# Attention and mixing kernel: a tile's keys in one stretch of 160 columns, its values in two transfers, and a new written order

## The chip, the cores and the metric

The kernel runs on one core of one Trainium2 chip. The metric is the device time of one execution in microseconds (us), as a median over runs; one execution was also taken with the hardware profiler. TensorE is called PE here, its weight loads PEld, VectorE DVE, ScalarE ACT, GpSimd POOL and SyncE SP.

## What is computed

Sparse attention over batch 4, heads 8, sequence 768, head size 64, then a mixing block on the result:

```python
k_sum = k.reshape(B, H, nb, block, D).max(axis=3)        # block 32, nb 24
v_sum = v.reshape(B, H, nb, block, D).mean(axis=3)
mask_l = np.abs(pos[:, None] - pos[None, :]) < window    # window 16
scores_s = scale * np.einsum('bhsd,bhnd->bhsn', q, k_sum) + np.log(block)
scores_all = np.concatenate([scores_l_m, scores_s], axis=-1)
...
x = attention output, (B, S, H * D)
theta = x @ w_theta
yr = np.einsum('ts,bsd->btd', w_tok_r, x * np.cos(theta))
yi = np.einsum('ts,bsd->btd', w_tok_i, x * np.sin(theta))
u = x + yr + yi
out = u + np.maximum(u @ w_ch, 0.0)
```

A query sees its 15 neighbours on each side and the 24 block summaries; all else is masked away.

## The kernel before

The work is laid down as a list of operations, one after the other with what each reads and writes: the attention prepass of a batch (`prepass`: maxima of the keys on DVE, sums of the values by matmuls or by DVE), 24 attention tiles of 128 queries (`att_tile`), the theta product and the sines of each tile (`theta_tile`), the mix over tokens (`mix_step` for batches 0 and 1, `mix_fast` with seven products for batches 2 and 3) and the channel product (`out_batch`). PE runs these in turn; attention and theta of later tiles lie between mix products of earlier ones. Before any of it PE multiplies zeros for some 7.6 us (L381).

The order is not found at run time: `ORDER` (L54 to L143) names every operation by its number, in the order of issue, with a letter where another engine than the cheapest takes it (d DVE, g POOL). Each engine takes its instructions in the order of that list, and SP issues all transfers in it, one after the other, waiting for each one's buffer.

One attention tile takes two halves (g) of 64 queries. A half sees 24 block summaries and NL local keys, its 64 queries with HALO 15 on each side, 94 in all, so NK is 118. In `att_tile` (L481) the tile `k` holds for each of 4 head pairs and both halves these 118 columns, and behind them the queries. For batch 0 the local keys are copied from the whole keys in on-chip memory (`zu`, L506), one copy for each half and each two pairs; for batches 1 to 3 one transfer from `qg` brings local keys and queries (L529). The summaries are copied in at L515 and L519. The values `v` come in one transfer (L498) with both halves side by side; their 24 summaries stand above them, copied at L501. Then come the scores on PE (L538, two PSUM tiles `s`), the masked minimum on DVE (L574), the exponential on ACT (L578), a transpose on PE of each half's rows (L587), a copy of the turned weights `e` by ACT or DVE (L593), the product with `v` on PE (L561), and the division (L602 to L611). The PSUM tiles `pa` are shared by value sums, transposes and block products, so these wait for each other's copies.

The value sums of batch 0 are twelve matmul records at L452, from three transfers `x<-vn`; ACT copies the result at L475 (`vs`). The theta weights (`wth`) arrive as 64 bit floats and are turned to 32 bit ones in five steps (L403 to L414) on ACT, POOL and DVE, into tiles `xl` and `xh`; then they are scaled (L1031, L1032). Lines L763 are sums of quarters, on `f` for weights and on `zu` for the mix of batches 2 and 3.

Of the kernel before, what the change touches and what calls it, by code (L numbers as in the profile page):

```python
# [23 lines left out]
HALO = WIN - 1  # L24
# [6 lines left out]
VL = 96  # L31
# [23 lines left out]
27 23 25 15 31 39 17 24 29 99 44 28 33 0g 1g 2 35 78 3 45 4 186 40 85 26 193 43 8g 5 6g 9 30 10 11g 18 19 7g 194 20 21 22 32  # L55
12 48g 47 14 46 49 50 13 190g 237g 100 101g 34 239 59 63 235 51 60 52 64 61 65 238g 192 36 92 54 58 56 53 79 55 102 62 187 57
103 37 38g 104 105d 66 691d 67 80 81 82 42g 188g 83 191 68 195 41 291g 69d 70 196 189g 240g 84 71 86 87g 293 199 106 107 198
197 204 206 294g 207 200 203 205 685g 241 72 75d 289 73 210 76 208 74d 202 77d 88 93 223 236 201 211 209 347g 242 245 249 94
224 243 244 345g 247 89 212 213 215 214 246 225 248 216 117 95 220 90 96 91d 97 346g 250 397 348g 98 226 217d 251 252 108 253
218 221 254 227 256 219d 118g 292g 222d 122 119 228 123 255 258 257 124 229 230 689g 120 259 260 295 261 296 269 121 262 419g  # L60
125 231 109 298 270 263d 232 302 126 233 398 266 343 264 271 304 405 272 687g 273 274 290 399 128 692g 307 267 281 265d 311
268d 275 297 306 110 282 305 299 421g 301 309 276 349 285g 300 303 310 406 308 129g 350 352 234g 353 312 130 277 354 131 313
283 323 315 400 111 416 314 133 316 351 358 409 324 325 420 418 284 360 287g 278 317 362 134g 355 135 356 364 132 326 136 327
357 359 363 137 328 279g 344 401 288g 280 361 365 329 320d 403 422 318 321 319d 322d 410 431 366 367 138 686g 434 438 330 433
335 368d 337 331 417 377 688g 402 432 601g 369 332 404 378d 370 116 139g 338 476 690g 423 426 430 477 371d 374d 424 372 437
375 379 425 429 373d 376d 380 140 411 381 334 407 141 428 142 286g 113 16 427 439 436 435 527 440 441 442 478 602 382 172
333g 412 443 383 479 482 408 528 447d 444d 487 445 489 336 143 491 389 144g 448 112 384 173g 446 449d 488 524 486 490 153 413
494 493 145 414 174 146 492 114 391 450 473 483 480 484 481 485 415g 529 147 495 525 115 148 390 175 385 526 392 149g 386 154
475 127 451d 530 474 150 496 155 497 151 498 452 176 453 454 455 152 156 158 387 157 456 499 177 727 533 457 500 532 388g
503d 572 501 504 159g 178 538 458 459 502d 464 460g 506 466 540 505d 165 467 507 539 508 693 509 537 531 535 510 536 543 534  # L70
160 541 542 545 694 544 697 511 695 728 166g 167 179 462 512 161 546 547 168 573 162 169 696 463g 465 163 180 698 549 513 170
548d 164 514 515 699 181 171 550 182 516 518 608 522 554 183 523 700g 393 519 520 184 729 521 574 551 517g 575 561 341g 607
582 584 394g 576 461g 559 731 588 701 555 702 185 585 730 637 571 580 560 733 562 557 719 552 553 577 558g 732 579 581 703
1238 563 583 556 768 578 713g 734 569 565 771 589 586 342 609 339g 340g 769 590 587 720 567 591 592 704 564 638g 735 593 603
# [207 lines left out]
def attn_moe(tc, qg, vg, kT, vT, vn, wth, wtr, wti, wch, out, tune=TUNE):  # L282
# [69 lines left out]
    for g in range(2):  # L352
        local = lambda g=g: masks(slice(g * QT, (g + 1) * QT), slice(NB, NK))
        keep(local, [[0, 3], [1, NL]], 3 * NL, 0, -1, ALU.is_ge, far, (cs, "mask"))
        keep(local, [[0, 3], [-1, NL]], 3 * NL, 2 * HALO, 1, ALU.is_ge, far, (cs, "mask"))
# [798 lines left out]
```

## Time and profile before

| what | us |
|---|---|
| median of 3 runs | 426.37 |
| lowest, highest | 426.08, 429.6 |
| the profiled execution | 425.32 |
| its span, first to last instruction | 423.6 |
| PE, PEld, DVE, ACT, POOL busy | 413.3, 343.9, 356.3, 298.1, 207.4 |

The profiled execution's own time is the one to compare with sums made from its rows; its span is what the views cover. A matmul's end is modelled, so where PE counts as busy it may still not be at its pace; the start of the next run of matmuls says how long one took. An engine's idle time matters where PE waits behind it.

### The profile page before, as it was taken

The numbers are of one execution on the slowest core, as the hardware profiler recorded it, in microseconds if no ns is written. First come the engines' busy times: TensorE is split into PE (matmuls) and PEld (weight loads), VectorE is DVE, ScalarE is ACT, GpSimd is POOL, SyncE is SP. The second block draws the span as 40 slices with busy tenths as digits, with TensorE's granted clock in tenths as the row PEclk, the third lists the DMA queues.
The fourth block names the chain that finished last, engine by engine and source line by source line (L and its number), as shares of the span: only waits on it lengthen the run. The fifth ranks groups of instructions, "written<-read, shape, count | busy, mean of one in ns | idle before, by whom it ended". The sixth has DMA issues, their size and how long they took to land.

```text
span 423.6 us, 10058 instructions
## 1 busy us (share of the span) xinstructions
PE 413.3 (98%) x3626; PEld 343.9 (81%) x3626; DVE 356.3 (84%) x963; ACT 298.1 (70%) x609; POOL 207.4 (49%) x211
## 2 busy tenths in 40 slices
PE   8789999999999999999999999999999999999996
PEld 3356666578888888888888899898889999999996
DVE  3799999998797896787778787776887899999996
ACT  2899999997588886878779976685564547465230
POOL 3435562329833545875755876835515411133241
PEclk9999999999999999999999999999999999999999
DMA  8999799567869799777896998998788599111355
GB/s 294 351 351 319 256 384 285 157 212 193 273 181 245 177 261 277 223 241 230 227 271 166 310 248 244 303 267 249 182 242 336 192 349 305 50 39 45 124 209 183
DMA packets 95234, 100.07 MB, mean 236 GB/s; under 512 B 41936, under 2 KB 80848, under 8 KB 95184
## 3 DMA queue, kind: packets, MB, share of 16 engines
q1 hardware_dynamic: 95184, 99.43, 76.0%
q8 instruction: 28, 0.46, 0.4%
q14 instruction: 22, 0.18, 0.1%
HBM read 75.82 MB, written 23.59 MB: 235 GB/s over the span
## 4 chain that ended last, share of the span: by engine, by line
PE 88%; DVE 7%; ACT 2%; issue 1%; DMA 1%; DVEq 0%; SPq 0%; ACTq 0%
PE m L735 23%; PE m L851 20%; PE t L677 11%; PE c L956 6%; PE pa L561 6%; PE m L956 5%; PE s L538 5%; PE t L672 4%; PE pa L587 3%; PE t L381 2%; PE t L956 1%; DMA v<-vg 1%; DVE e L574 1%; DVE x L975 1%; DVE f L763 1%
## 5 line engine op out<-in xcount | busy, mean ns | idle before, releaser
L851 PE MATMUL m<-wt,hl 128*128 128x384 f32 x504 | 93.0, 339 | 0.3
L851 PEld LDWEIGHTS m<-wt,hl 128*128 128x128 f32 x504 | 87.2, 188 | 3.5 <-issue 0.5
L735 PE MATMUL m<-wt,hl 128*128 128x512 f32 x480 | 89.4, 340 | 0.0
L735 PEld LDWEIGHTS m<-wt,hl 128*128 128x128 f32 x480 | 74.2, 188 | 11.6 <-issue 0.3
L578 ACT ACTIVATE e<-e,st 128x118 f32<-128x118 f32 x192 | 64.4, 389 | 10.6 <-DVE st L574 7.3
L574 DVE CUSTOM_DVE_ANT_0 e<-s,cs 128x118 f32<-128x118 f32 x192 | 45.6, 271 | 7.1 <-PE pa L561 4.5
L320 POOL TENSOR_TENSOR hl<-zu,hl 128x512 fp32r<-128x512 f32 x24 | 33.1, 1386 | 27.8 <-ACT hl L311 8.5
L677 PE MATMUL t<-wth,xh 128*128 128x512 f32 x144 | 45.8, 399 | 0.0
L707 POOL TENSOR_TENSOR zu<-xn,zu 128x512 f32<-128x512 f32 x24 | 32.9, 1381 | 21.2 <-DVE wt L414 10.0
L311 ACT CAST hl<-zu 128x512 fp32r<-128x512 f32 x43 | 26.1, 619 | 16.4 <-PE m L851 9.9
L561 PEld LDWEIGHTS pa<-v,e 118*64 118x64 f32 x768 | 24.6, 137 | 9.7 <-issue 3.4
L320 DVE TENSOR_TENSOR hl<-zu,hl 128x512 fp32r<-128x512 f32 x38 | 28.3, 751 | 3.0 <-ACT hl L311 2.9
L561 PE MATMUL pa<-v,e 118*64 118x65 f32 x768 | 28.0, 224 | 2.7 <-ACT xh L1031 1.0
L677 PEld LDWEIGHTS t<-wth,xh 128*128 128x128 f32 x144 | 25.2, 188 | 4.5
L677 PE MATMUL t<-wth,xl 128*128 128x512 f32 x72 | 28.4, 394 | 0.0
L763 POOL TENSOR_TENSOR zu<-zu 128x512 f32<-128x512 f32 x14 | 18.8, 1357 | 16.2 <-DVE hl L320 10.9
L763 POOL TENSOR_TENSOR f<-f 128x192 f32<-128x192 f32 x26 | 17.4, 670 | 18.2 <-DVE f L763 11.2
L538 PE MATMUL s<-k 64*64 64x118 f32 x768 | 25.7, 266 | 0.6 <-PE pa L561 0.6
L593 ACT COPY e<-pa 118x512 f32<-118x512 f32 x30 | 16.7, 584 | 13.4 <-PE pa L587 13.4
L578 ACT ACT_TABLE_LOAD x18 | 23.1, 1283 | 2.7 <-DVE st L574 2.5
L700 ACT ACT_TABLE_LOAD x19 | 24.4, 1283 | 0.3
L593 DVE COPY e<-pa 118x512 f32<-118x512 f32 x18 | 12.2, 688 | 14.5 <-PE pa L587 8.4
(181 smaller groups left out, 891.0 us busy)
## 6 DMA issues: line engine op xcount, KB each, us to landing
wt<-s_scratch SPq DMA_DIRECT2D x48, 384.0 KB, 5.1
k<-qg SPq DMA_DIRECT2D x18, 632.0 KB, 5.7
v<-vg SPq DMA_DIRECT2D x24, 390.0 KB, 5.5
s_scratch<-f SPq DMA_DIRECT2D x24, 384.0 KB, 3.5
wt<-wtr SPq DMA_DIRECT2D x6, 768.0 KB, 10.5
wt<-wti SPq DMA_DIRECT2D x6, 768.0 KB, 11.7
f<-kT SPq DMA_DIRECT2D x12, 384.0 KB, 3.6
f<-vT SPq DMA_DIRECT2D x12, 384.0 KB, 4.8
```

The source lines that it names most:

```text
L320: lambda e: V[e].tensor_tensor(dst(), src(), hi().bitcast(F32), op=ALU.subtract), reads, writes, due, port=BOTH)
L538: mm(0.79 * len(pairs) / NP, [lambda p=p, g=g, h=h: nc.tensor.matmul(sc[h].get()[ROW[g], p], q()[ROW[h], p, ROW[g]], keys_of()[ROW[h], :, ...
L561: mm(2 * 0.433 + scores[0] + (0.2 if scores[0] else 0.0), [lambda n=n, g=g, a=a: nc.tensor.matmul(xa[a].get()[ROW[g], n], turned[g].get()[ ...
L574: op({"DVE": 0.205}, lambda eng, n=n: nc.vector.tensor_tensor_reduce(e()[:, n], sc[n % 2].get()[:, 2 * a + n // 2], mask(m), -SCALE, 3.0e3 ...
L578: op({"ACT": 0.288}, lambda eng, n=n: nc.scalar.activation(e()[:, n], e()[:, n], AF.Exp, bias=st.get()[:, n:n + 1], scale=-1.0), [(st, n)] ...
L593: lambda e, t=t, g=g: (nc.scalar.copy if e == "ACT" else nc.vector.tensor_copy)(t.get()[:NK], tp[g].get()[:NK].rearrange("k n q -> k (n q) ...
L677: calls = [lambda t=t, xx=xx, k=k, c=c: nc.tensor.matmul(th.get(), xx.get()[:, c], w_th[c].get()[:, k], start=(c == 0 and t == 0), stop=(c ...
L707: op({"DVE": c_dve(DM, "two"), "POOL": c_pool(DM)}, lambda e, z=z, hc=hc: V[e].tensor_tensor(z(), xn[b, i].get().rearrange("p h d -> p (h ...
L735: nc.tensor.matmul(acc[th](), zz, w[:, TT[th]], start=(s == 0 and r == 0 and t == 0 and (th == 0 or c == 0)), stop=(s == NT - 1 and r == 1 ...
L763: lambda e: V[e].tensor_tensor(dst(), x(), y(), op=ALU.add if sign > 0 else ALU.subtract), reads, writes, due, port=BOTH)
L851: calls = [lambda ref=ref, tt=tt, z=z, s=s, j=j, t=t, x=x, k=k, bank=bank, first=first: nc.tensor.matmul(bank[j].get()[:, :HT], z.get()[:, ...
L956: calls = [lambda k=k, t=t, x=x, y=y: nc.tensor.matmul(to.get(), weights[n][x][0]()[:, k, j * P:(j + 1) * P], operands[n].get()[:, y, k], ...
```

## The change

HALO becomes 16, so a half has 96 local keys and NK is 120. The two halves' local keys overlap, and the tile now holds them once: for each head pair 24 summaries, 160 local keys and 24 summaries again. Half 0 reads summaries and the first 96 local keys, half 1 the last 96 and the summaries behind them (L536 of the changed kernel). For half 1 the summaries now stand behind the local keys, and in `v` it is half 0 that has them behind, so the masks are built anew (two more fills). Batch 0 needs one copy of local keys for each two pairs and not two; batches 1 to 3 have one transfer for the keys and one for the queries. The values of each half come in a transfer of their own, straight to the rows of that half. The arrays in memory are laid out to match.

`ORDER` is written anew; in the list of operations 31 more stand. The words of the change say that instruction packets were in the reckoning by which the order was found: that reckoning is not part of the program.

```diff
-HALO = WIN - 1
+HALO = WIN
-VL = 96
+LW = P + 2 * HALO
+KW = 2 * NB + LW
 ORDER = """
-27 23 25 15 31 39 17 24 29 99 44 28 33 0g 1g 2 35 78 3 45 4 186 40 85 26 193 43 8g 5 6g 9 30 10 11g 18 19 7g 194 20 21 22 32
+24 25 26 27 28 29 9g 18g 0g 12g 10 11 1 30 40 45 2 3g 4 5 19 6g 31 7g 32 34 78 46 36 92 48g 186 41 20 43 21 22 23 49 85 47 50
...
-    fill(lambda: masks(every, slice(0, NB)), math.log(BLK) / SCALE, 3 * NB, (cs, "mask"))
-    fill(lambda: masks(every, slice(NB, NK)), 0.0, 3 * NL, (cs, "mask"))
+    fill(lambda: masks(every, slice(0, NK)), 0.0, 3 * NK, (cs, "mask"))
...
+        at = (0, NL)[g]
+        fill(lambda rows=rows, at=at: masks(rows, slice(at, at + NB)), math.log(BLK) / SCALE, 3 * NB, (cs, "mask"))
...
-            vbuf[b] = [Ref(apool, [NB + VL, 2, H, DV], tag="v", bufs=K["VB"]) for _ in range(K["VB"])]
+            vbuf[b] = [Ref(apool, [NK, 2, H, DV], tag="v", bufs=K["VB"]) for _ in range(K["VB"])]
...
-        KE, LE = NK * 2 * NP, 2 * NP * NL
+        KE, LE = KW * NP, LW * NP
...
-        dma(lambda: v.get()[NB:], lambda: vg[b, i], 2 * H * (VL + 16) * DV * 4, [], [(v, "loc")], due, 4160, 0.35)
+        local, blocks = ((NB, 0), (0, NL))
         for g in range(2):
+            dma(lambda g=g: v.get()[local[g]:local[g] + NL, g], lambda g=g: vg[b, 2 * i + g], H * NL * DV * 4, [], [(v, ("loc", g))], due, 2080, 0.35)
...
-                    if len(r) == NP:
-                        to(keys_of()[:, :NB // 2].rearrange("p u (a g) w -> p (u a) g w", g=2),
-                           ks.get().rearrange("p u a w -> p (u a) w")[:, :, None].broadcast_to((P, NP * NB // 2, 2, 2)))
-                    else:
-                        for g in range(2):
-                            to(pieces(slice(0, NB // 2), pp, g), ks.get()[:, :, pp])
+                    for first in (0, (KW - NB) // 2):
+                        to(keys_of()[:, first:first + NB // 2, pp], ks.get()[:, :, pp])
...
-                    for g in range(2):
-                        w = slice((2 * i + g) * QT, (2 * i + g) * QT + NL)
-                        copy(lambda g=g, h=h: pieces(slice(NB // 2, NK // 2), slice(2 * h, 2 * h + 2), g), lambda h=h, w=w: keys[0][h].get()[:, :, w].rearrange("p a (u w) -> p u a w", w=2),
-                             2 * NL, [(keys[0][h], x) for x in (2 * h, 2 * h + 1)], [(k, (x, g)) for x in (2 * h, 2 * h + 1)])
+                    w = slice(i * P, i * P + LW)
+                    copy(lambda h=h: keys_of()[:, NB // 2:(KW - NB) // 2, 2 * h:2 * h + 2], lambda h=h, w=w: keys[0][h].get()[:, :, w].rearrange("p a (u w) -> p u a w", w=2),
+                         2 * LW, [(keys[0][h], x) for x in (2 * h, 2 * h + 1)], [(k, (x, "loc")) for x in (2 * h, 2 * h + 1)])
...
-            dma(lambda: qk.get()[:, KE - LE:], lambda: qg[b, i], (LE + NP * P) * 512, [],
-                [(k, "q")] + [(k, (x, g)) for x in range(NP) for g in range(2)], due, (LE + NP * P) * 4)
+            dma(lambda: qk.get()[:, NB * NP:NB * NP + LE], lambda: qg[b, i][:, :LE], LE * 512, [], [(k, (x, "loc")) for x in range(NP)], due, LE * 4)
+            dma(lambda: qk.get()[:, KE:], lambda: qg[b, i][:, LE:], NP * P * 512, [], [(k, "q")], due)
...
-                sc[h].get()[ROW[g], p], q()[ROW[h], p, ROW[g]], keys_of()[ROW[h], :, 2 * p + g], start=True, stop=True)
-                for p in pairs for g in range(2) for h in range(2)], [(k, "q")] + [(k, (x, y)) for x in pairs for y in ("sum", 0, 1)], [(x, y) for x in sc for y in pairs], due, mode="score")
+                sc[h].get()[ROW[g], p], q()[ROW[h], p, ROW[g]], keys_of()[ROW[h], g * (KW - NK) // 2:(g * (KW - NK) + NK) // 2, p], start=True, stop=True)
+                for p in pairs for g in range(2) for h in range(2)], [(k, "q")] + [(k, (x, y)) for x in pairs for y in ("sum", "loc")], [(x, y) for x in sc for y in pairs], due, mode="score")
```

How the order moves is shown at two places. The first is SP at the start of the program, whose rows are transfers in the order of issue: `zu<-kT` are the keys of a head pair of batch 0, `k<-qg` a tile's queries, `x<-vn` values for the sums, `wth` theta weights, `v<-vg` a tile's values. Before:

```order
L305 DMA zu<-kT 128x798 x3
L305 DMA x<-vn 128x2x512
L305 DMA k<-qg 128x512
L305 DMA zu<-kT 128x798
L305 DMA wth_91<-wth 128x1024
L305 DMA x<-vn 128x2x512 x2
L305 DMA wth_103<-wth 128x1024
L305 DMA k<-qg 128x512
L305 DMA v<-vg 96x1040
L305 DMA wth_116<-wth 128x1024
```

Now:

```order
L307 DMA zu<-kT 128x800 x4
L307 DMA k<-qg 128x512
L307 DMA x<-vn 128x2x512 x2
L307 DMA wth_119<-wth 128x1024
L307 DMA x<-vn 128x2x512
L307 DMA wth_123<-wth 128x1024
L307 DMA k<-qg 128x512
L307 DMA v<-vg 96x520 x2
L307 DMA wth_145<-wth 128x1024
```

The fourth key transfer stood behind a value transfer and a query transfer and now follows the third; both value transfers move behind it by one or two places; a tile's values are two rows of half the width.

The second is DVE behind the softmax of tile 0 (its last rows are the ISA ones, the masked minimum and its sum). `xl` and `xh` are theta weights on their way to 32 bits, `pa` the turned weights of tile 0. Before:

```order
L574 ISA st 128x1
L411 SCALAR_TENSOR_TENSOR xl<-wth_91,xl 128x512
L414 SCALAR_TENSOR_TENSOR xl<-wth_91,xl 128x512
L1032 TENSOR_SCALAR xl<-xl 128x512
L313 CAST wth_218<-xl 128x512
L407 TENSOR_SCALAR xh<-xh 128x512
L409 TENSOR_SCALAR xh<-xh 128x512
L411 SCALAR_TENSOR_TENSOR xh<-wth_103,xh 128x512
L414 SCALAR_TENSOR_TENSOR xh<-wth_103,xh 128x512
L593 COPY e<-pa_220 118x512
L574 ISA e,st<-s_245,cs 128x118
L574 ISA st 128x1
```

Now:

```order
L573 ISA e,st<-s_135,cs 128x120
L573 ISA st 128x1
L409 TENSOR_SCALAR xh<-wth_119 128x512
L411 TENSOR_SCALAR xh<-xh 128x512
L413 TENSOR_SCALAR xh<-xh 128x512
L415 SCALAR_TENSOR_TENSOR xh<-wth_119,xh 128x512
L418 SCALAR_TENSOR_TENSOR xh<-wth_119,xh 128x512
L411 TENSOR_SCALAR xh<-xh 128x512
L481 MEMSET vs 24x8
L1031 TENSOR_SCALAR xh<-xh 128x512
L413 TENSOR_SCALAR xh<-xh 128x512
L506 COPY v<-vs 24x520
L592 COPY e<-pa_225 120x512
```

The copy `e<-pa` stood behind two whole chains on `xl` and `xh` and a cast; now it stands behind one chain and the first steps of the second, with a copy of value sums (`v<-vs`) in front of it that DVE did not have.

## Rows read from the trace of the kernel before

**Rows 1.** The page's busy times, whole span

```profile
PE 413.3 (98%) x3626; PEld 343.9 (81%) x3626; DVE 356.3 (84%) x963; ACT 298.1 (70%) x609; POOL 207.4 (49%) x211
```

**Rows 2.** Stages: us, busy PE, PEld, DVE, ACT, POOL, clock, DMA share, GB/s

```profile
9.00:37.40 28.40, 24.47 (x310) 13.36 (x310) 24.49 (x94) 25.04 (x61) 10.78 (x24) 1.00 0.99 340
37.40:87.00 49.60, 49.60 (x481) 29.77 (x479) 48.20 (x151) 48.55 (x102) 24.61 (x25) 1.00 0.81 268
90.30:238.80 148.50, 148.11 (x1503) 124.49 (x1502) 120.81 (x378) 118.11 (x258) 89.61 (x87) 1.00 0.82 230
355.20:416.70 61.50, 61.50 (x355) 61.33 (x354) 59.97 (x96) 28.06 (x47) 21.20 (x12) 1.00 0.33 116
416.70:423.60 6.90, 3.31 (x20) 2.99 (x18) 3.88 (x8) 0.00 (x0) 0.00 (x0) 1.00 0.49 178
```

**Rows 3.** PE's waits, whole span: us, times, longest us

```profile
PE pa L561 <- ACT xh L1031: 1.0, 1, 1.0
PE pa L561 <- DVE e L593: 0.9, 2, 0.5
PE pa L587 <- ACT vs L475: 0.8, 1, 0.8
PE pa L561 <- issue: 0.6, 1, 0.6
PE s L538 <- PE pa L561: 0.6, 1, 0.6
```

**Rows 4.** Timeline of the head: start us, us, instructions, idle before

```profile
5.14 2.67 DVE L448 TENSOR_REDUCE ks<-zu 128x24 f32<-128x768 f32 x3 [3.63 <-DMA zu<-kT]
8.10 0.34 SPq L305 DMA_DIRECT2D v<-vg  x1
9.75 0.95 DVE L448 TENSOR_REDUCE ks<-zu 128x24 f32<-128x768 f32 x1 [1.94 <-DMA zu<-kT]
10.90 1.07 PE L538 MATMUL s<-k 64*64 64x118 f32 x32
12.41 3.61 PE L452 MATMUL pa<-x,vt 128*24 128x512 f32 x8 [0.44 <-DMA x<-vn]
18.66 0.68 DVE L593 COPY e<-pa 118x512 f32<-118x512 f32 x1
19.45 1.24 PE L561 MATMUL pa<-v,e 118*64 118x65 f32 x32 [0.97 <-ACT xh L1031]
37.38 1.02 PE L735 MATMUL m<-wt,zu 128*128 128x512 f32 x2
```

**Rows 5.** Groups by shape: count, busy us, mean ns

```profile
L593 DVE COPY e<-pa 118x512 f32<-118x512 f32 x18 | 12.2, 688 | 14.5 <-PE pa L587 8.4 <-ACT zu L688 5.9
L763 DVE TENSOR_TENSOR zu<-zu 128x512 f32<-128x512 f32 x16 | 12.1, 762 | 0.2
L763 DVE TENSOR_TENSOR f<-f 128x192 f32<-128x192 f32 x22 | 9.4, 429 | 0.8 <-POOL f L763 0.7
L506 POOL COPY k<-zu 128x188 f32<-128x188 f32 x13 | 5.0, 393 | 11.1 <-DMA zu<-kT 4.2 <-DVE xh L414 3.1 <-DVE wt L414 2.3
L506 ACT COPY k<-zu 128x188 f32<-128x188 f32 x11 | 3.6, 357 | 1.9 <-DMA zu<-kT 1.7 <-PE s L538 0.2
```

**Rows 6.** Chain that ended last: start us, us, what

```profile
60.37 0.97 PE s L538 x32
104.04 1.05 PE m L735 x6
143.91 1.25 PE m L735 x6
238.94 3.13 PE m L851 x18
```

**Rows 7.** DMA issues: count, KB each, median us to landing

```profile
v<-vg SPq DMA_DIRECT2D x24, 390.0 KB, 5.5
out<-x SPq DMA_DIRECT2D x16, 192.0 KB, 2.2
```

More of the change, by code (lines that the diff above doesn't have):

```diff
@@ L143 @@
+2347 2299 2344 2324 2315g 2327 2350 2335 2325d 2345 2295 2331 2320g 2348d 2336 2332 2333 2346 2352 2351 2353 2339 2278 2337
+2340 2354 2356 2334 2357 2358 2338 2360 2341 2355 2361 2359 2362
 """
@@ L497, in att_tile @@
         v = vbuf[b][i % K["VB"]]
-        dma(lambda: v.get()[NB:], lambda: vg[b, i], 2 * H * (VL + 16) * DV * 4, [], [(v, "loc")], due, 4160, 0.35)
+        local, blocks = ((NB, 0), (0, NL))
         for g in range(2):
+            dma(lambda g=g: v.get()[local[g]:local[g] + NL, g], lambda g=g: vg[b, 2 * i + g], H * NL * DV * 4, [], [(v, ("loc", g))], due, 2080, 0.35)
             if i < K["VB"]:
                 op({"POOL": c_pool(H * DV, False), "ACT": c_act(H * DV), "DVE": c_dve(H * DV, "fast")}, lambda e, g=g: (
-                    nc.scalar.copy if e == "ACT" else V[e].tensor_copy)(v.get()[:NB, g], vs.get()), [vs], [(v, ("sum", g))], due, port=BOTH)
+                    nc.scalar.copy if e == "ACT" else V[e].tensor_copy)(v.get()[blocks[g]:blocks[g] + NB, g], vs.get()), [vs], [(v, ("sum", g))], due, port=BOTH)
         k = qk
@@ L507, in att_tile @@
         parts = [range(0, 2), range(2, 4)] if b * NT + i < K["SP0"] else [range(NP)]
-        pieces = lambda u, pp, g: keys_of()[:, u].rearrange("p u (a g) w -> p u a g w", g=2)[:, :, pp, g]
         for r in parts:
@@ L520, in att_tile @@
                 n = 2 * len(r) * NB
-                op({"POOL": c_pool(n, False), "ACT": c_act(n)}, sums_copy, [(ks, x) for x in r], [(k, (x, "sum")) for x in r], due, port=BOTH)
+                op({"POOL": c_pool(n, False) + 0.25, "ACT": c_act(n) + 0.2}, sums_copy, [(ks, x) for x in r], [(k, (x, "sum")) for x in r], due, port=BOTH)
             if b == 0:
                 for h in range(r.start // 2, (r.stop + 1) // 2):
-                    for g in range(2):
-                        w = slice((2 * i + g) * QT, (2 * i + g) * QT + NL)
-                        copy(lambda g=g, h=h: pieces(slice(NB // 2, NK // 2), slice(2 * h, 2 * h + 2), g), lambda h=h, w=w: keys[0][h].get()[:, :, w].rearrange("p a (u w) -> p u a w", w=2),
-                             2 * NL, [(keys[0][h], x) for x in (2 * h, 2 * h + 1)], [(k, (x, g)) for x in (2 * h, 2 * h + 1)])
+                    w = slice(i * P, i * P + LW)
+                    copy(lambda h=h: keys_of()[:, NB // 2:(KW - NB) // 2, 2 * h:2 * h + 2], lambda h=h, w=w: keys[0][h].get()[:, :, w].rearrange("p a (u w) -> p u a w", w=2),
+                         2 * LW, [(keys[0][h], x) for x in (2 * h, 2 * h + 1)], [(k, (x, "loc")) for x in (2 * h, 2 * h + 1)])
@@ L1118, in _layout @@
     qg = qT.reshape(B, NP, P, NT, P).transpose(0, 3, 2, 1, 4).reshape(B, NT, P, NP * P)
-    kg = np.stack([kp[..., j * QT:j * QT + NL] for j in range(NG)], 3)
-    kg = kg.reshape(B, NP, P, NT, 2, NL // 2, 2).transpose(0, 3, 2, 5, 1, 4, 6).reshape(B, NT, P, 2 * NP * NL)
-    vg = np.zeros((B, NG, VL, H, DV), np.float32)
+    kg = np.stack([kp[..., j * P:j * P + LW] for j in range(NT)], 3)
+    kg = kg.reshape(B, NP, P, NT, LW // 2, 2).transpose(0, 3, 2, 4, 1, 5).reshape(B, NT, P, NP * LW)
+    vg = np.zeros((B, NG, NL, H, DV), np.float32)
     vg[..., D:] = 1.0
```

186 lines of the change are left out of this document (93 added, 93 removed), and 6 rows, old and new, of the table ORDER.

## The prediction

> **What bounds the kernel now.** I read the page's busy times first. TensorE (PE) is busy for 413.3 of 423.6 us [rows 1]; nothing else comes near. The stages say where the other 10.3 us are [rows 2]: between 9.00 and 37.40 us PE is busy for 24.47 of 28.40, so 3.93 us are missing there; in the tail from 416.70 on 3.31 of 6.90 (3.59 missing, the last results on their way out, which the change doesn't touch); from 37.40 to 87.00 and from 355.20 to 416.70 nothing is missing. The list of PE's waits names the same places [rows 3]: waits of 0.6 to 1.0 us for the first tiles (the block product for ACT 1.0, the row transposes for ACT's copy of the value sums 0.8, scores for the block product 0.6, one 0.6 with no cause shown), and two waits of 0.5 at most, 0.9 together, of a block product for DVE's copy of the turned weights. The granted clock is 1.00, the 2.4 GHz level, in every stage [rows 2], so it takes and gives nothing.
>
> So this change can win only where PE waits, in the head above all, and can lose wherever it makes PE wait or gives it more to do. Shorter work on ACT, GpSimd (POOL) or DVE is worth nothing by itself.
>
> **PE's own work, part by part.** The matmuls are the same in number; what changes is width and neighbours. Score matmuls go from 118 to 120 columns. A tile's 32 score records run off in 0.97 us [rows 6]; 24 tiles by 0.97 by 2/118 is **+0.4 us**. The smaller stride of the keys that PE reads has no row; I take zero for it. In the block product the contraction is 120 rows and not 118, with 65 columns moved as before: zero. The softmax passes grow by the same 2 columns on DVE and ACT, beside PE's work: zero.
>
> Counted in the two orders, PE leaves its long products for the attention pieces (scores, row transposes, block product) 42 times and not 40. Six mix matmuls take 1.05 us in the middle of long products and 1.25 behind an attention piece [rows 6]: 0.2 per visit, so **+0.4 us** (0 if the new neighbours are cheaper, 0.6 if dearer).
>
> **The head.** Four terms of the head's order can be followed. First, SP now issues all four key transfers of batch 0 before anything else. Before, DVE's reductions of the first three ran without a pause from 5.14 for 2.67 us, and the fourth waited until 9.75 [rows 4], with its issue three transfers further back. With all four in front the fourth should land by about 7.8 (three had landed by 6.9 or so), its reduction ends near 5.14 + 4 x 0.89 = 8.7, and the first scores can start when the warm-up ends, near 9.3 (its zeros are now written by POOL, behind another fill), and not at 10.90 [rows 4]. But the value-sum products come behind them, and the last of these still needs the third value transfer, for which PE waited until 12.41 [rows 4], with the same bytes ahead of it as now: they end at about 15.5 and not 16.0, so 0.5 us of the 0.8 wait for the value sums is left as gain. Second, DVE's copy of the turned weights stood behind two chains on the weights and began at 18.66; the block product followed at 19.45 [rows 4] and PE had idled 1.0 [rows 3]. Now it stands ahead of most of the second chain: the copy can follow the transposes at about 17.5 and the block product the scores, near 17.8. That is the 1.0 us. Third, the copies of the local keys fall from 24 of 188 columns (0.357 us on ACT, 0.393 on POOL [rows 5]) to 12 of 320; at a width-proportional 0.61 to 0.67 that is 9.0 us before and some 7.7 after, one or two us less on engines of which ACT is busy for 25.04 of 28.40 us there [rows 2]. The sum copies take some of it back, two instructions each where most had one. It helps the others and is no term. Fourth, half of theta tile 1 moves ahead of the third block product: the same work in another order.
>
> Sum for the head: 0.5 + 1.0 = **-1.5 us**, provided that it reaches the first mix product, at 37.38 before [rows 4]. Bounds: 0, if a later chain on ACT takes it all, and -3.9, if all of PE's idle time goes.
>
> **The later stages.** The two waits for DVE's copy, 0.9 us [rows 3], stand at places where the order is now another. Nothing says that their successors are better or worse: between -0.9 and +0.9, and I take half of the first, **-0.45**. The one wait without a shown cause, 0.6 [rows 3], is what instruction packets could explain; they are in the planner's reckoning, not in the program, so I count nothing for them.
>
> **Transfers.** A tile's values come in two transfers, keys and queries in two where batches 1 to 3 had one: 24 + 18 = 42 issues more, at the 0.34 us of a value issue [rows 4] 14 us of SP's time, spread over the span. What is added is a wait: a block product waits for both value halves, a score product for keys and queries, and PE takes its instructions in order, so all its work queues behind. The cover is long: the first values were issued at 8.10 and used at 19.45 [rows 4] and take 5.5 us to land [rows 7]. A second half that is 0.34 us late costs nothing as long as that cover stands; without it, 24 x 0.34 = 8 us. Bytes fall by 18 x 56 KB, 1.0 MB. For the landing of half a transfer beside others there is no row; the nearest are 192 KB to the output in 2.2 us and 390 KB of values in 5.5 [rows 7]. Two halves of 195 KB, one behind the other, would by these take from 4.4 us, 1.1 less than now, to 11.0, 5.5 more. I take the value in between that stands in a row, 5.5: no change.
> The Trainium skill (DMA: Bandwidth & Descriptors, section Bandwidth) speaks against the split: efficiency grows with size, and transfers should be gathered to 1 MiB or more. The trace does not show that loss: 192 KB landed in 2.2 us where 390 KB took 5.5 [rows 7]. By the rule the landings in the head would come later and the second rival below would be the outcome.
>
> **Sum.** -1.5 - 0.45 + 0.4 + 0.4 = -1.15 us. The profiled execution took 425.32 us, 1.7 around its span; that makes 424.2. It lay 1.05 below the median of the runs, 426.37, so on that scale **425.2 us**. With the ends of each term, without the extreme of the head, 422.8 to 428.0.
>
> **Rivals.**
> *All the idle time goes.* The new order closes the head (-3.9) and both later waits (-0.9), against +0.4 for the columns, and groups visits as cheaply as now: -4.4, or 422.0, just over 1% faster. For it: three of four engines have less to do in the head. Against it: the third value transfer is a floor at 12.4, and DVE and ACT are busy for 24.5 and 25.0 of 28.4 us there [rows 2].
> By the Trainium skill (Perfetto Trace Analysis, section Identifying the Most-Contended Engine) busy matmul time is a poor measure of room, and the weight load's is better. Weight loads are busy for 124.49 of 148.50 us in the long middle, 61.33 of 61.50 in the channel stage [rows 2], which would leave room for more gain in the middle. Against that, 18 mix matmuls without a neighbour took 3.13 us [rows 6], 174 ns each; an order does not change that pace.
>
> *The order does not do what it says in the head, since transfers bound it.* The DMA engines are at 0.99 in 9.00 to 37.40, at 340 GB/s [rows 2]: landings move little by an issue that comes earlier, and the weight transfers that come later make up for it. The head's 1.5 and the 0.45 are void: +0.8, or 427.2.
>
> *DVE becomes the bound: slower.* Counted in the orders, DVE gets six more of the 762 ns sums on zu, three more of the 688 ns copies, and seven fewer of the 429 ns sums on f [rows 5]: 4.6 + 2.1 - 3.0 = 3.7 us more, and with the other shifts perhaps twice that, 7.4. From 37.40 to 87.00 it is busy for 48.20 of 49.60 us [rows 2], room for 1.4. If the most of it falls there PE waits for 7.4 - 1.4 = 6.0 us: 426.37 - 1.5 + 0.8 + 6.0 = 431.7. It decides once DVE has more than 1.4 us more to do in that stretch. Against it: the sums on zu belong to the stages behind it, and the channel stage has 1.5 us of room (59.97 of 61.50).
>
> **How the numbers follow.** A measurement of this kernel can tell about 1% from no change, that is below 422.1 or above 430.6. Forecast 0.55; all idle time gone 0.18; transfers bound the head 0.15; DVE the bound 0.12. Faster by over 1%: most of the first rival and the edge of the forecast, 0.18. Slower: most of the last, 0.11. Within 1%: 0.71. The range that leaves out half of the first rival and most of the last is 421.0 to 429.5.
>
> **What would show it.** Right: the four key reductions without a pause; first scores near 9.3; the first block product near 17.8; the first mix near 35.9; idle time of PE in the head near 2.4 and not 3.9; a tile's scores in 0.99. Wrong: a wait of a block product for a value transfer or of scores for q; DVE above 99% between the first mix and 87 us with PE waiting for it; the first mix still near 37.4 (then transfers bound the head), or a block product that has waits after most attention tiles.

## The result, and the profile after

The changed kernel takes 430.87 us (median of 8 runs, 430.72 to 432.33) where the kernel before took 426.57 beside it (8 runs, 425.21 to 429.9): a ratio of 1.0098, 95% interval 1.0076 to 1.0121. It is slower by 4.2 us. The forecast was 425.2, which was 1.15 below the median of before. The profiled execution took 430.75 us, its span is 429.0.

The page's busy times, against [rows 1]: PE has 4.4 us more, DVE 7.1 more, ACT 8.8 less.

```profile
PE 417.7 (97%) x3626; PEld 346.7 (81%) x3626; DVE 363.4 (85%) x971; ACT 289.3 (67%) x586; POOL 203.5 (47%) x211
```

The stages of [rows 2], in the same stretches. In the head PE has lost another half us (4.47 missing and not 3.93). From 37.40 to 87.00 it is full as before, and DVE has less to do there (47.62 us, before 48.20), so DVE is not the bound. In the long middle 0.73 us are missing, before 0.39. The clock is at its upper level, 1.00, throughout.

```profile
9.00:37.40 28.40, 23.93 (x306) 12.99 (x307) 23.51 (x98) 22.19 (x55) 8.59 (x16) 1.00 1.00 330
37.40:87.00 49.60, 49.60 (x481) 30.02 (x479) 47.62 (x147) 48.78 (x98) 24.96 (x23) 1.00 0.90 278
90.30:238.80 148.50, 147.77 (x1483) 123.92 (x1487) 121.33 (x368) 109.56 (x232) 92.84 (x96) 1.00 0.82 226
```

PE's waits, against [rows 3]. The two waits for DVE's copy of turned weights and the wait for ACT's weight chain are gone; the scores of tile 3 now wait 1.3 us, the first scores 0.7 for q.

```profile
PE s L537 <- DVE vt L472: 1.3, 1, 1.3
PE pa L586 <- ACT vs L479: 0.9, 1, 0.9
PE s L537 <- DVE st L573: 0.7, 1, 0.7
PE pa L586 <- ACT e L577: 0.7, 2, 0.4
PE s L537 <- DMA k<-qg: 0.7, 1, 0.7
```

The head, against [rows 4]. DVE's four reductions come in two pairs. The first scores start at 9.34, the last value-sum products end at 16.52 (14.62 + 1.90; before 12.41 + 3.61 = 16.02), the first block product starts at 19.05, the scores of tile 3 at 31.48, the first mix product at 38.66 (before 37.38). SP issues the third value transfer at 5.30 (before at 4.7), with the same transfers ahead of it as before: four of keys, one of queries, two of values, one of theta weights (4.27). The last row is PE's last product.

```profile
4.47 1.90 DVE L452 TENSOR_REDUCE ks<-zu 128x24 f32<-128x768 f32 x2 [4.47 <-DMA zu<-kT]
7.55 1.96 DVE L452 TENSOR_REDUCE ks<-zu 128x24 f32<-128x768 f32 x2 [1.17 <-DMA zu<-kT]
...
4.27 0.98 SPq L307 DMA_DIRECT2D wth<-wth  x1
5.30 0.65 SPq L307 DMA_DIRECT2D x<-vn  x1
...
9.34 1.27 PE L537 MATMUL s<-k 64*64 64x120 f32 x32 [0.69 <-DMA k<-qg]
14.62 1.90 PE L456 MATMUL pa<-x,vt 128*24 128x512 f32 x4 [0.41 <-DMA x<-vn]
19.05 1.15 PE L560 MATMUL pa<-v,e 120*64 120x65 f32 x32
31.48 1.10 PE L537 MATMUL s<-k 64*64 64x120 f32 x32 [1.34 <-DVE vt L472]
38.66 4.09 PE L734 MATMUL m<-wt,zu 128*128 128x512 f32 x12
...
425.19 0.34 PE L955 MATMUL m<-wt,xh 128*128 128x384 f32 x1
```

Half a tile's values lands in 4.4 us where the whole took 5.5 [rows 7]:

```profile
v<-vg SPq DMA_DIRECT2D x48, 195.0 KB, 4.4
```

Not every half comes that soon. The halves of tile 6's values are issued at 64.09 and 64.99 and land after 7.6 and 9.9 us, at 71.7 and 74.9. PE begins the block product at 74.74, before the second half is there, and is through it at 76.11: 1.37 us where 1.08 is usual, 0.3 us that the list of waits does not name.

```profile
64.99 0.60 SPq L307 DMA_DIRECT2D v<-vg  x1
...
v<-vg SPq DMA_DIRECT2D x1, 195.0 KB, 9.9
...
74.74 1.44 PE L560 MATMUL pa<-v,e 120*64 120x65 f32 x32
76.11 1.12 PE L671 MATMUL t<-xh,x 128*128 128x512 f32 x2
```

Two points of the section on the change read otherwise in the kernels. In `v`, as in the keys, it is half 1 that has the summaries behind its local rows, and half 0 has them ahead. And of the three value transfers of batch 0 only the first moves back, behind the queries; the second comes one place earlier and the third keeps its place.

Head and body are told apart below by one measure: the body runs from the start of the first mix product to the start of PE's last product, and holds the same number of matmuls (3308) with either order and either layout. For the changed kernel it is 425.19 - 38.66 = 386.5 us. Several expectations speak of idle time over pace: the same stretch less its matmuls at their undisturbed pace, a sum of mine over the runs of matmuls in the trace. Differences of the two measures agree to some tenths, but for the channel stage, which only the first holds to its end. Line numbers differ by two or three among the kernels.

### The profile page after: what moved, and what is told of

The parts are those of the page before. It is cut to its first block, busy times and chain, and to the rows that moved or that the text cites. A ratio compares the mean times of both kernels' runs of the same rounds, so it can differ in the third digit from the quotient of the medians.

```text
span 429.0 us, 10125 instructions
## 1 busy us (share of the span) xinstructions
PE 417.7 (97%) x3626; PEld 346.7 (81%) x3626; DVE 363.4 (85%) x971; ACT 289.3 (67%) x586; POOL 203.5 (47%) x211
## 4 chain that ended last, share of the span: by engine, by line
PE 85%; DMA 8%; DVE 4%; ACT 2%; issue 1%; SPq 0%; DVEq 0%
PE m L734 23%; PE m L850 19%; PE t L676 12%; PE c L955 7%; PE pa L560 6%; PE m L955 5%; PE s L537 5%; PE t L671 4%; PE pa L586 3%; DMA f<-vT 3%; DMA v<-vg 2%; DMA k<-qg 2%; DMA wt<-s_scratch 1%; PE t L955 1%; PE t L637 1%
## 5 line engine op out<-in xcount | busy, mean ns | idle before, releaser
L577 ACT ACTIVATE e<-e,st 128x120 f32<-128x120 f32 x192 | 64.0, 387 | 16.3 <-DVE st L573 15.3
L573 DVE CUSTOM_DVE_ANT_0 e<-s,cs 128x120 f32<-128x120 f32 x192 | 45.5, 273 | 10.8 <-PE pa L560 7.9
L560 PEld LDWEIGHTS pa<-v,e 120*64 120x64 f32 x768 | 25.1, 137 | 7.6 <-issue 4.7
L762 POOL TENSOR_TENSOR f<-f 128x192 f32<-128x192 f32 x33 | 22.4, 677 | 16.1 <-DVE f L762 3.7
L537 PE MATMUL s<-k 64*64 64x120 f32 x768 | 27.0, 273 | 2.8 <-DVE vt L472 1.3
L560 PE MATMUL pa<-v,e 120*64 120x65 f32 x768 | 28.6, 224 | 0.4 <-ACT e L592 0.2
L537 PEld LDWEIGHTS s<-k 64*64 64x64 f32 x768 | 21.0, 132 | 7.7 <-issue 4.7
L706 DVE TENSOR_TENSOR zu<-xn,zu 128x512 f32<-128x512 f32 x26 | 19.3, 752 | 4.4 <-ACT zu L700 4.4
L734 PE MATMUL m<-wt,zu 128*128 128x512 f32 (+1 forms) x64 | 23.0, 495 | 0.0
L592 ACT COPY e<-pa 120x512 f32<-120x512 f32 x27 | 15.4, 583 | 10.3 <-PE pa L586 10.2
```

What stands on the lines that cost most here:

```text
L537: mm(0.79 * len(pairs) / NP, [lambda p=p, g=g, h=h: nc.tensor.matmul(sc[h].get()[ROW[g], p], q()[ROW[h], p, ROW[g]], keys_of()[ROW[h], g * ...
L560: mm(2 * 0.433 + scores[0] + (0.2 if scores[0] else 0.0), [lambda n=n, g=g, a=a: nc.tensor.matmul(xa[a].get()[ROW[g], n], turned[g].get()[ ...
L573: op({"DVE": 0.205}, lambda eng, n=n: nc.vector.tensor_tensor_reduce(e()[:, n], sc[n % 2].get()[:, 2 * a + n // 2], mask(m), -SCALE, 3.0e3 ...
L577: op({"ACT": 0.288}, lambda eng, n=n: nc.scalar.activation(e()[:, n], e()[:, n], AF.Exp, bias=st.get()[:, n:n + 1], scale=-1.0), [(st, n)] ...
L706: op({"DVE": c_dve(DM, "two"), "POOL": c_pool(DM)}, lambda e, z=z, hc=hc: V[e].tensor_tensor(z(), xn[b, i].get().rearrange("p h d -> p (h ...
L734: nc.tensor.matmul(acc[th](), zz, w[:, TT[th]], start=(s == 0 and r == 0 and t == 0 and (th == 0 or c == 0)), stop=(s == NT - 1 and r == 1 ...
```

## Experiments

A table first. Ratios are to the kernel before, timed beside each; the first mix and the body are those of the profiled execution.

| kernel | ratio (95%) | first mix | body |
|---|---|---|---|
| before | 1 | 37.38 | 382.3 |
| before_again | - | 39.98 | 382.4 |
| changed kernel | 1.0098 (1.0076-1.0121) | 38.66 | 386.5 |
| after_again | 1.0102 (1.0067-1.0136) | 40.63 | 387.0 |
| layout_alone | 1.0001 (0.9978-1.0025) | 37.47 | 383.5 |
| order_alone | 1.0062 (1.0036-1.0088) | 39.52 | 386.2 |
| width_alone | 1.0003 (0.9981-1.0025) | 39.81 | 383.5 |
| stretch_of_4 | - | 38.26 | 382.7 |
| stretch_of_8 | 0.9983 (0.9960-1.0005) | 38.34 | 383.0 |
| reduction_later | 1.0118 (1.0088-1.0148) | 39.01 | 387.2 |
| values_behind_q | 1.0155 (1.0119-1.0190) | 38.93 | 389.5 |
| old_head_new_body | 1.0160 (1.0131-1.0190) | 39.70 | 390.6 |
| body_repairs | 1.0071 (1.0046-1.0097) | 38.98 | 385.4 |
| body_repairs_2 | 1.0056 (1.0034-1.0079) | 39.02 | 384.9 |
| new_order_all_repairs | 1.0039 (1.0017-1.0061) | 38.38 | 385.8 |
| old_order_stretch_8 | 0.9959 (0.9939-0.9979) | 37.01 | 382.7 |

**Layout or order?** The change has two halves, the layout with its split transfers and the order. Each was put alone into the other kernel; the order is carried over instruction by instruction.

```diff
 layout_alone: layout, copies and transfers of the changed kernel
-order of the changed kernel
+order of the kernel before
 order_alone: layout, copies and transfers of the kernel before
-order of the kernel before
+order of the changed kernel
```

> The new layout and the split transfers with the order of before, carried over instruction by instruction (each pair of local-key copies stands where the first of the two stood, each split transfer where the whole one stood). Theory 'the order costs most': the change lost 4.3 us, of which the slower scores (24 tiles x 0.06 us) are 1.4; without the new order only these are left, so 427.5 to 428.5, first mix near 37.4, the wait of the scores of tile 3 (1.3) gone. Rival 'layout and splits cost most' (more transfers in a full queue, q behind keys, two halves of values): 430 to 431, with block products or scores waiting for transfers, and the first mix at 38.5 or later.

> The old layout and whole transfers with the order of after, carried over in the same way. Theory 'the order costs most': 429 to 430 (4.3 us less the 1.4 of the scores), first mix near 38.7, scores of tile 3 waiting about 1.3 us near 30, scores 0.97 per tile. Rival 'layout and splits cost most': 426 to 427, first mix at 37.4 or earlier.

layout_alone came out at 1.0001, order_alone at 1.0062: the order carries the larger part. layout_alone has no wait for a value transfer or for q in its body, so with the old order the splits cost nothing that shows; with the new order they do, in one place (below). Its scores take 1.03 us per tile, and its body is 1.2 us longer than before, about what 20 tiles behind the first mix by 0.06 make. That its time doesn't show these 1.2 us (0.28%, just above the interval's end) stays open; its head, with fewer copies and bytes, may give them back. order_alone loses 2.65 us (0.62% of 427), and its body alone is 3.9 longer (386.2 - 382.3).

**Why are the scores slower?** width_alone has the two columns and the old interleaved keys. stretch_of_4 and stretch_of_8 have the new layout and the old order, with the keys of a head pair in longer runs, so that a matmul steps over 64 or 128 bytes and not 32.

```diff
 width_alone (in the kernel before)
-HALO = WIN - 1
+HALO = WIN
-    keep(local, [[0, 3], [1, NL]], 3 * NL, 0, -1, ALU.is_ge, far, (cs, "mask"))
+    keep(local, [[0, 3], [1, NL]], 3 * NL, -1, -1, ALU.is_ge, far, (cs, "mask"))
...
 stretch_of_8 (in layout_alone, and so in the copies and the host's layout; stretch_of_4 with 4)
-        keys_of = lambda: qk.get()[:, :KE].rearrange("p (u c w) -> p u c w", c=NP, w=2)
+        keys_of = lambda: qk.get()[:, :KE].rearrange("p (u c w) -> p u c w", c=NP, w=8)
```

> The kernel before with a halo of 16 and not 15: scores of 120 columns, keys still in the old interleaved layout, order and transfers unchanged. Theory 'the stretch of both halves (smaller stride, both halves reading the same keys) slows the scores': 0.985 us per tile and not 1.03, the period of a group of four score matmuls at 104 ns and not 110, and 426.5 to 427.2. Rival 'the width does it': 1.03 per tile, 110 ns, 427.7 to 428.3.

> Order of before, new layout, but the keys of a head pair in runs of 4 floats and not of 2, so that score matmuls step over 64 bytes as in the kernel before and not over 32. Theory 'the smaller step slows the scores': 0.99 per tile. Rival 'both halves reading the same keys slows them': 1.03 per tile.

> As stretch_of_4 with runs of 8 floats, steps of 128 bytes. Theory 'the smaller step': 0.99 or less per tile, so 24 x 0.04 = 1.0 us under the kernel with the new layout and the old order, ratio to before 0.997 to 0.999. Rival 'the same keys': 1.03 per tile, ratio 1.000.

The scores of tile 14 in four kernels, from their start to the start of the block product behind them. width_alone, 1.00:

```profile
169.66 1.07 PE L538 MATMUL s<-k 64*64 64x120 f32 x32
170.66 1.15 PE L561 MATMUL pa<-v,e 120*64 120x65 f32 x32
```

layout_alone, 1.03:

```profile
167.53 1.10 PE L535 MATMUL s<-k 64*64 64x120 f32 x32
168.56 1.15 PE L558 MATMUL pa<-v,e 120*64 120x65 f32 x32
```

stretch_of_8, 0.98:

```profile
168.26 1.05 PE L535 MATMUL s<-k 64*64 64x120 f32 x32
169.24 1.15 PE L558 MATMUL pa<-v,e 120*64 120x65 f32 x32
```

Before it was 0.97 [rows 6]. So the columns cost 0.02 to 0.03 per tile (the rest of width_alone's longer body is 0.5 us in which the fast mix waits for a transfer), and the short runs at the small step another 0.03 to 0.05. The rival falls: in stretch_of_4 (0.98 in all its tiles) and stretch_of_8 both halves read the same keys too. Whether it is the step or the run can be told from the four kernels only this far: runs of two floats are nearly free at a step of 64 bytes and not at 32.
The Trainium skill (SBUF — State Buffer, section Door 1: The DMA port swizzle) says that SBUF has lines of 16 bytes and that two accesses to a line are enough for full bandwidth. By that rule runs of two floats would cost the same at either step; the runs show 1.03 against 1.00, and the measurement decides.

**Is the head's 1.3 us the order's?** First the kernel before once more.

```diff
 before_again: no change
```

> The kernel before, unchanged, for a second profile. Theory 'the head is bound by transfers and its end moves from one execution to the next': the first mix product starts at another time than 37.4, by up to 2 us, with the same instructions, and the span moves with it, while the idle time over pace behind the first mix stays within 0.5 us of 16.4. Rival 'the head's 1.4 us belong to the new order': the first mix again between 37.2 and 37.6.

The same program starts its first mix 2.6 us later, and its body is the same to 0.1 us (422.36 - 39.98 = 382.4):

```profile
39.98 2.74 PE L735 MATMUL m<-wt,zu 128*128 128x512 f32 x8
...
422.36 0.34 PE L956 MATMUL c<-wt,xh 128*128 128x384 f32 x1
```

Over all profiles the first mix starts between 37.01 and 39.98 in the eight kernels with the old head (mean 38.5) and between 38.38 and 40.63 in seven with the new one (mean 39.2, without values_behind_q). A difference of 0.7 between such spreads is not settled, and one profile of each kernel could not have shown 1.5 us either way.

Then the wait of the scores of tile 3. The chain of the changed kernel comes to it through the reduction of a value transfer that was issued at 18.73:

```profile
18.73 11.78 DMA f<-vT
30.51 0.02 issue
30.53 0.96 DVE vt L472
31.50 1.08 PE s L537 x32
```

But q of that tile was issued at 19.99, by SP's timeline, and its transfer took 11.4 us, by the DMA issues from 15 to 35 us, which is to 31.4:

```profile
19.99 0.33 SPq L307 DMA_DIRECT2D k<-qg  x1
...
k<-qg SPq DMA_DIRECT2D x1, 256.0 KB, 11.4
```

Two moves tell the two apart.

```diff
 reduction_later, on DVE
-vt <- f (L472); ...; 8 softmax passes of tile 3 (L573)
+...; 8 softmax passes of tile 3 (L573); vt <- f (L472)
 values_behind_q, on SP and DVE
-f <- vT; q of tile 3; values; ...; f <- kT; f <- kT
+q of tile 3; values; ...; f <- kT; f <- kT; f <- vT (its reduction moved back as well)
```

> The changed kernel with one instruction moved: DVE's reduction of the first transfer of transposed values (L472, of batch 1), which the trace names as the cause of the 1.3 us for which the scores of tile 3 wait, stands behind the softmax of tile 3. Its transfer is issued where it was. Theory A 'DVE's order makes the scores of tile 3 wait': they start near 30.2 and not 31.5, the first mix near 37.5, and 1.3 us are back (ratio to before near 1.007). Theory B 'the transfer of q of tile 3 is what they wait for' (issued 19.99, 11.4 us to land, 31.4): they start at 31.4 as before, the wait is now named DMA k<-qg, and the time stays (ratio 1.009 to 1.010).

> The changed kernel with the first transfer of transposed values of batch 1 (384 KB) issued behind q of tile 3 and the values of the next tile, and its reduction moved back with it; nothing else. Theory B: the 384 KB are off the way of q, at some 316 GB/s 1.2 us, so q lands near 30.2, the scores of tile 3 start there and the first mix near 37.5: 1.2 us back, ratio near 1.007. Theory A: the same, since the reduction is gone as well. Rival C 'the queue is full whatever its order': q lands at 31 or later, as other transfers move up, and the ratio stays at 1.009 to 1.010.

In reduction_later the scores of tile 3 wait as before, and the wait is now named for q:

```profile
31.83 1.10 PE L535 MATMUL s<-k 64*64 64x120 f32 x32 [1.18 <-DMA k<-qg]
```

order_alone, too, names q for its wait at this place, 1.5 us. In values_behind_q q lands at 30.9 (issued at 20.32, 10.6 us) and not near 30.2; the scores follow at 31.02, the step behind them waits for the theta chain on DVE, and the first mix starts at 38.93:

```profile
31.02 1.09 PE L535 MATMUL s<-k 64*64 64x120 f32 x32
32.70 0.66 PE L635 MATMUL t<-cs,xn 128*128 128x128 f32 x4 [0.58 <-DVE zu L687]
```

Theory A falls: q was the cause. Of the 1.2 us that both theories gave about 0.4 came. From the last theta product ahead of the scores to the first mix it is 9.05 us (29.88 to 38.93), and 9.54 and 9.40 in the two profiles of the changed kernel; behind q the chain through DVE is nearly as late. That the first mix is no earlier lies in what came before: this execution was 0.8 us later at that theta product. The reductions that were pushed back then cost 3 us of body (389.5), so the ratio of 1.0155 lies above all three expectations. A wait named for an engine whose work ended at the same moment as a transfer (31.48 and 31.4) was the transfer's.

**Head or body, by a seam.** The order of before to the first mix, that of after behind it:

```diff
 old_head_new_body
-order of the changed kernel
+order of before up to the first mix product; then the order of the changed kernel
```

> The new layout and split transfers with the order of before up to the first mix product, that of after behind it. Theory 'most of the order's cost lies behind the head' (idle over pace in the body 19.8 and 20.2 us in the two kernels with the new order, 16.4 and 17.5 in the two with the old one): about 2.7 us over the kernel with the old order throughout, ratio 1.006 to 1.007. Rival 'the head is the cost' (scores of tile 3 waiting for q): ratio 1.000 to 1.003.

1.0160, worse than either. It can't tell: the seam leaves softmax work undone that the new order counts on, and PE waits there in one place for longer than the whole effect. The stretch from 38 to 56 us:

```profile
PE pa L558 <- DVE e L590: 1.9, 1, 1.9
```

**The body.** The trace of after shows one long gap behind 187 us. PE has 30 mix products at 174 ns, to 192.46, begins the row transposes of tile 15 at 193.12 and needs 1.06 for them where 0.61 is usual: 1.1 us lost. order_alone, with the old layout, loses as much at the same place (last row: 30 mix products from 188.18 leave off near 193.40, the transposes take until 195.16); layout_alone, with the old order, loses nothing there.

```profile
185.06 1.10 PE L537 MATMUL s<-k 64*64 64x120 f32 x32
186.10 1.21 PE L560 MATMUL pa<-v,e 120*64 120x65 f32 x32
187.24 5.57 PE L734 MATMUL m<-wt,hl 128*128 128x512 f32 x30
193.12 1.13 PE L586 MATMUL pa<-cs,e 64*120 64x64 f32 x16 [0.32 <-ACT e L577]
...
194.11 1.12 PE L585 MATMUL pa<-cs,e 64*118 64x64 f32 x16 [0.46 <-DVE x L752]
```

ACT does sine and cosine first, then loads the table of the exponentials, then all eight:

```profile
188.98 0.72 ACT L699 ACTIVATE zu<-zu,bright 128x512 f32<-128x512 f32 x1
189.61 0.62 ACT L700 ACTIVATE zu<-zu 128x512 f32<-128x512 f32 x1
190.23 1.28 ACT L577 ACT_TABLE_LOAD   x1
191.53 2.40 ACT L577 ACTIVATE e<-e,st 128x120 f32<-128x120 f32 x8
```

Between the end of a tile's scores and its row transposes PE has other work, the cover of the softmax. For tile 15 this cover was 15.8 us in the old order (177.7 to 193.5) and is 7.0 in the new (186.1 to 193.1), the wait of 0.7 included; the last exponential ends at 193.9. Its mean over the 20 tiles behind the head is the same (11.5 and 11.8). A short cover is not enough to lose time: tile 17 of the kernel before has 5.5 us (214.52 to 219.98), and its transposes take the usual time. Its exponentials start at 216.13, 1.6 us behind the scores, with no table load ahead of them; those of tile 15 in the changed kernel start 5.4 us behind, at 191.53.

```profile
214.52 1.15 PE L561 MATMUL pa<-v,e 118*64 118x65 f32 x32
...
219.98 0.71 PE L587 MATMUL pa<-cs,e 64*118 64x64 f32 x16
```

Two smaller pauses of the changed kernel stand at 145 (a block product behind ACT's copy) and 275.

```diff
 body_repairs
 ACT near 189
-sin, cos (L699, L700); 8 exponentials of tile 15 (L577); e <- pa (L592)
+8 exponentials of tile 15 (L577); e <- pa (L592) x2; sin, cos (L699, L700)
 ACT near 145
-zu <- zu (L693); e <- pa (L592)
+e <- pa (L592); zu <- zu (L693)
 DVE near 275
-first softmax pass of tile 22 (L573); zu <- zu,t (L689)
+zu <- zu,t (L689); first softmax pass of tile 22 (L573)
 body_repairs_2, besides
 DVE near 189
-ks <- f (L452); softmax passes of tile 15
+softmax passes of tile 15; ks <- f (L452)
 ACT near 189
-exponentials of tile 15 in the order of after
+exponentials of tile 15 in the order of their softmax passes
```

> The changed kernel with five instructions moved behind the head: ACT's sine and cosine chain near 189 us behind the eight exponentials and the two copies of the turned weights of tile 15 (as in the order of before) and one DVE product that reads it; ACT's step ahead of the copy of the turned weights near 145 behind it; DVE's first softmax pass of tile 22 behind the step of theta that PE waits for near 275. Theory 'single places in ACT's and DVE's queues cost the body its time': the pauses near 187 and 193 (0.67 and 0.69 over pace), 145 (0.5) and 275 (0.44) go, 2.2 us in all, ratio near 1.0045. Rival 'they only move on' (the same work is late next at another place): the four pauses go, others of the same size come, ratio 1.008 to 1.010.

> The repairs of body_repairs and two more moves for tile 15: DVE's reduction of a key transfer (L452) behind the softmax passes of the tile, and ACT's exponentials in the order in which these passes come (ACT waited 1.15 us for the pass of the one that stands first, before it loaded its table). Theory 'single places': the pauses near 187 and 193 (0.53 and 0.69) go too, idle over pace in the body falls from 19.1 to 18, and the ratio from 1.0071 to 1.0045. Rival 'they move on': the pauses go but come at the next tile, body still 19 or more, ratio 1.007.

body_repairs: the pauses at 145 and 275 went, that of tile 15 stayed. ACT now waits for a softmax pass, and loads its table only behind that wait:

```profile
190.15 1.28 ACT L575 ACT_TABLE_LOAD   x1 [1.15 <-DVE st L571]
```

So each theory was half right. body_repairs_2 brings the load forward by one us and the pause is gone, with a cover of tile 15 of 6.5 us and not 7.0, though a block product near 198 now loses 0.4:

```profile
189.11 1.28 ACT L575 ACT_TABLE_LOAD   x1
```

The body falls from 386.5 by 1.1 and then 0.5, the ratio from 1.0098 to 1.0071 and 1.0056; two profiles of the changed kernel differ by 0.5 as well (386.5 and 387.0), so the second step by itself is not settled. Of the 2.6 us that are left of its body 1.2 are the scores and 0.5 the block product of tile 6.

**Do the parts add up?**

```diff
 new_order_all_repairs: body_repairs_2
-keys in runs of 2 floats
+keys in runs of 8 floats
 after_again: no change to the changed kernel
 old_order_stretch_8: stretch_of_8, and on DVE
-a weight chain's step, ..., zu <- zu,t; e <- pa of tile 7
+e <- pa of tile 7; the weight chain's step, ..., zu <- zu,t
-x <- m,x (L753); e <- pa of tile 11
+e <- pa of tile 11; x <- m,x (L753)
```

> The changed kernel with keys in runs of 8 floats and all moves of body_repairs_2. Theory 'the loss is the scores' step (24 x 0.05 = 1.2 us) and single places in the body (ratio 1.0056 with those of body_repairs_2 mended), and nothing else of size': ratio 1.002 to 1.004, scores 0.98 per tile, body idle over pace near 17.8. Rival 'something not seen yet costs 2 us': ratio 1.005 or more.

> The changed kernel, unchanged, beside the other two. Both theories: ratio 1.008 to 1.012, scores 1.03 per tile, body idle over pace within 0.5 us of 20.2; the first mix product within 2 us of 38.8, since the head's end moves from one execution to the next.

> Order of before, new layout in runs of 8 floats, and two of DVE's copies of turned weights moved ahead (tile 7's ahead of a step of a weight chain, tile 11's ahead of an addition into x), for which a block product waited 0.49 and 0.43 us. Theory 'what an order loses here are single copies late in a queue': both pauses go, body idle over pace 16.1 and not 17.0, ratio 0.996 to 0.997, the fastest version. Rival 'they move on': ratio 0.998 to 0.999 as stretch_of_8.

On one chip the changed kernel is at 1.0102 and the mended one at 1.0039: the scores' step and the moved instructions hold 0.63%, 2.7 of the 4.3 us. Its body is longer than forecast, since PE waited for two transfers:

```profile
PE pa L558 <- DMA v<-vg: 0.8, 1, 0.8
PE m L848 <- DMA wt<-s_scratch: 0.6, 1, 0.6
```

The first is the block product of tile 6, which waits for the second half of its values, a sign the prediction named for split transfers. It is no accident of this execution. The product takes 2.13 us here, 1.37 and 1.73 in the two profiles of the changed kernel, 1.40 and 1.57 in the two with body repairs; 1.08 is usual. PE goes on 0.1 to 0.2 us behind the landing of that half: here it was issued at 64.58 and landed after 10.7 us, and PE went on at 75.41; in after_again it landed at 77.3 and PE went on at 77.40, and there the wait is named for DVE. layout_alone, with the same halves in the old order, has no such wait, nor has order_alone, whose whole transfer landed at 74.2 for a product at 75.43. So new order and split together cost 0.3 to 1.0 us at this place. That is read from the traces; no run joins the halves in the changed kernel.

Against stretch_of_8 (0.9983), which differs from it in the order alone, the mended order is still 2.4 us behind. In the profiles its body is 2.8 longer (385.8 and 383.0), of which the two waits are 1.4; what the rest is stays open.

old_order_stretch_8 is the fastest: 0.9959 (0.9939 to 0.9979), 1.75 us below the kernel before. Its block products of tiles 7 and 11 follow at once. Against the expectation half of the first pause came back as a wait of the mix for a weight's low part (0.3), and the body is 0.3 shorter than in stretch_of_8; the rest of its lead lies in the head, which is not settled:

```profile
88.31 1.15 PE L558 MATMUL pa<-v,e 120*64 120x65 f32 x32
...
90.27 6.46 PE L732 MATMUL m<-wt,hl 128*128 128x512 f32 x34 [0.26 <-DVE wt L320]
```

## Why the prediction was wrong

**The step that failed is the one on the later stages** ("between -0.9 and +0.9, and I take half of the first, -0.45"). The two waits for DVE's copy did go. For all behind the first mix the forecast had 0.4 + 0.4 - 0.45 = +0.35 us; the body became 4.2 longer (386.5 against 382.3), as much as the whole loss of 4.2. The body of the changed kernel is 3.0 to 3.4 us longer than that of layout_alone (386.5 and 387.0 against 383.5), which differs from it in the order alone. The bound was drawn from the waits that one order happens to have, not from what another can have. The listing of the new order showed the place: on PE the row transposes of tile 15 stand 30 mix products behind its scores, where before two mix stretches (48 products) and theta products stood between, and on ACT sine and cosine stand ahead of the tile's exponentials. Five moved instructions and then two more took back 1.6 us of it (386.5 to 384.9), 0.5 of the rest is the block product of tile 6, and the last 0.9 stay open.

**The score term was too small.** +0.4 was taken from the width, with zero for the smaller stride, "which has no row". It is 24 x 0.06 = 1.4: the columns 0.5 to 0.7 by width_alone, the step the rest.

**The head's -1.5 did not come.** The scores started at 9.34, as forecast, but by luck: the zeros were through by 8.7 and PE waited 0.69 us for q, which had no term (in after_again it waited 2.02, until 10.12). The first part, 0.5, read the wait until 12.41 as one for the third value transfer. It was for the second: the third landed at 13.7 (issued at 4.7, 9.0 us) and its products followed without a pause. It has the same bytes ahead of it in the changed kernel, as the prediction says, but was issued at 5.30 and landed at 14.6, so the value sums ended 0.5 us later and not earlier. The second part, 1.0, came: the block product stands 1.6 us behind the row transposes (17.41 to 19.05), where it stood 2.7 behind (16.80 to 19.45). Behind that q of tile 3 was late, for which the prediction had no term. In before_again the value sums end at 16.97, later than in the changed kernel, and the block product stands 2.0 behind the transposes: with a swing of 2.6 us in one program, 1.5 us read from one profile was no ground for a term. The loss of 4.2 us is as large as the body's, so it leaves about nothing for the head; whether the order costs the head something is not settled.

**The transfers' zero was nearly right.** In the old order the split costs nothing that shows. But "A second half that is 0.34 us late costs nothing as long as that cover stands" fails for tile 6: its second half was issued 0.90 us behind the first and landed 3.2 us behind it, at 74.9 for a product that began at 74.74. That is 0.3 us in the changed kernel's profile and 0.65 in after_again, the sign of being wrong that the prediction named.

**Right:** DVE does not become the bound. The visits' +0.4 could not be told from the rest.

**The sum's ends.** With the ends of each term and without the extreme of the head the terms give -2.0 to +1.9, or 424.4 to 428.3, and not 422.8 to 428.0. The measured 430.87 lies outside both.

**The rivals.** "Transfers bound the head" is nearest: the first mix did not come earlier, and q is what PE waits for. Its 427.2 fell short because it too counted nothing for the body. The Trainium skill's rule that the prediction set beside it (DMA: Bandwidth & Descriptors, section Bandwidth: efficiency grows with size) would make a half the dearer per byte. The landings agree, 195 KB in 4.4 us and in 5.4 in layout_alone, 390 KB in 5.5 and in 5.2 in order_alone; no loss of time came of it in layout_alone (1.0001), which has all the splits. "DVE becomes the bound" had the right sign and the wrong mechanism: DVE has 7.1 us more to do in all, but less from 37.40 to 87.00. "All the idle time goes" fell.

## What to carry to other kernels

When an order is replaced, list for each tile the work that stands on the busiest engine between a producer and its consumer, and on the others what is queued ahead of the chain in between; a mean cover that stays the same says nothing, and the shortest one alone doesn't either: 5.5 us were enough where the exponentials began soon, 7.0 were not where sine, cosine and a table load stood ahead of them. Where a transfer is split, look for the consumer that stands closest behind the second half. Take two profiles of a kernel whose start is bound by transfers before a term is read from one: here the head moved by 2.6 us and the rest by 0.1. When operands move closer together, time the matmuls that read them; a layout that saves copies can cost the busiest engine more.

## What was not expected of the hardware

Score matmuls of 120 columns that read runs of two floats take 1.03 us per 32 at a step of 32 bytes, 1.00 at 64 bytes, and 0.98 with runs of four or eight floats. In body_repairs the table load of the exponentials stood behind the wait of the first of them: ACT sat idle 1.15 us and only then loaded for 1.28. Splitting 390 KB into two transfers of 195 KB changed no time that could be measured in the old order; in the new one two halves issued 0.90 us apart landed 3.2 us apart, and PE waited for the second.
